# A chain of relu-squared attention and two MLPs on one core: when score chunks are left out at block ends, and in which order tokens lie

## The chip, the cores and the metric

One core of a Trainium2 chip (trn2) runs the whole program in one launch. The metric is device time in microseconds (us). TensorE (PE) multiplies, with its weight loads shown as PEld; VectorE (DVE) and ScalarE (ACT) do the elementwise work; SyncE (SP) issues nearly all DMAs.

## What is computed

Inputs u, v (4 x 3072 x 256) and z (4 x 3072 x 64) and the weights are float32. The reference, cut to what matters:

```python
scores = np.matmul(z, z.transpose(0, 2, 1)) / S          # S = 3072, 4 batches
x = u * np.matmul(np.maximum(scores, 0.0) ** 2, v)       # attention
x_prev = shift(x, 1)                                     # along the sequence
xk, xr = mu_k * x + (1 - mu_k) * x_prev, mu_r * x + (1 - mu_r) * x_prev
k = np.maximum(xk @ w_k, 0.0)
y = sigmoid(xr @ w_r) * (k * k @ w_v)                    # channel mix
out = np.maximum(y @ w_in, 0.0) ** 2 @ w_out             # second MLP
```

## The kernel before, in words

Every matrix is split into a high part, rounded to the matmul's float32r, and a low part, the rest; a product is three matmuls (high by high, and the two mixed ones). Three parts run one after the other: attention, channel mix, second MLP. The change touches attention() alone.

Attention works through 24 **blocks** `n` (4 batches `b` of 6 blocks `ib`, 512 query tokens each). A block takes 24 **steps**, one for each **chunk** of 128 key tokens; four chunks make a key group `g`. A step attends one chunk: 12 matmuls of L406, eight that read the chunk's high part (ahi) and four that read its low part (alo). Since scores are symmetric, a chunk with g < ib isn't computed again: it was turned (transposed on DVE, L335) when the earlier block made it, stored to DRAM (turned, L340 and L342), and loaded back (mixed, L351 and L353). scores(s) makes chunk s. A computed chunk takes six matmuls (sps, L374) for each two chunks, then Relu (L357), Square (L378) and a copy to ahi (L381 or L383); a turned one takes only the copy to ahi (L366). The subtraction that makes alo is handed to finish(), which holds it back until the next chunk is made (L367 and L388). So the low part of the newest chunk is put into DVE's queue only with the chunk after it.

The order of all this is written out by hand in the loop at the end of attention(). At step s it makes chunks until `made` reaches s + 1 + `ahead`, then attends chunk s:

```python
ahead = 0 if j in (NJ - 3, NJ - 2) else min(LEAD, FIRST + max(0, s - 2 * NJ) // NJ)   # FIRST 4, LEAD 7, NJ 24
while made < min(n_steps, s + 1 + ahead):
    scores(made)
```

j is the step in its block. So chunks are made 4 ahead in blocks 0 to 2, then 5, 6 and 7 ahead in blocks 3, 4 and 5, and none is made at steps 21 and 22 of any block ("left out"). At step 23 the block ends: gate() moves its four sums out of PSUM (ACT L413 and L416, DVE L420 and L418) and multiplies by u (L427); only then are three chunks made at once. Everything else (loads and preparation of z, v, u, turned scores, pieces of weights) is hung on step numbers by at_step.

z is loaded turned: load_z issues DMAs of 64 KB in rows of 128 bytes (L255). For batches 1 to 3 it loads two, DVE transposes 64 partitions (L268), and a DMA within the chip copies them to the other 64 (zT<-zT, L270). ACT then copies zz from zT (L277). In blocks 2 to 4 of a batch, and for key groups 2 to 4 (`apart`), tokens lie in another order: v goes in four DMAs of 128 KB (L288), gate() writes through a permuted view, and turned scores with i >= 2 (`spread`) are stored in four DMAs of 256 KB (L340).

SP issues its DMAs in the order of the program, and an issue that has to wait holds up those behind it.

Of the kernel before, what the change touches and what calls it, by code (L numbers as in the profile page):

```python
# [16 lines left out]
Q = 32  # L17
# [4 lines left out]
def tile_relu2_attention__rwkv_channel_mix__relu2_mlp(  # L22
# [57 lines left out]
    turned = {k: dram.tile([R, R, Q, T] if s else [R, P, T], F32, name="turned%d_%d" % k) for k, s in spread.items()}  # L80
    apart = range(2, NB - 1)
# [160 lines left out]
    def attention():  # L242
        with ExitStack() as st:
# [9 lines left out]
            def load_turned(t, p, src, g, engine=nc.sync):  # L253

                engine.dma_start(out=t[p:p + Q].rearrange("q (k r) -> q k r", r=Q),  # L255
                                 in_=src.rearrange("(q k) r -> q k r" if g in apart else "(k q) r -> q k r", q=Q))

            def load_z(b, g, engines=None):
                z_raw[b, g] = t = io.tile([P, T], F32, tag="zn", name="zn")
                for k, e in enumerate(engines or (nc.sync,) * (R if b == 0 else R // 2)):  # L260
                    d = k * Q % DQ
                    load_turned(t, k * Q, z[b, g * T:(g + 1) * T, d:d + Q], g, e)

            def prep_z(b, g, stage):
                if stage == 0:
                    rows = slice(0, P if b == 0 else DQ)
                    zT[b, g] = t = io.tile([P, T], F32, tag="zT", name="zT", bufs=1)
                    nc.vector.transpose(t[rows], z_raw.pop((b, g))[rows])  # L268
                    if b > 0:
                        nc.sync.dma_start(out=t[DQ:P], in_=t[rows])  # L270
                    return
# [9 lines left out]
            def load_v(b, g):  # L281
                src = v[b, g * T:(g + 1) * T, :]
                if g not in apart:
                    load_raw(("v", b, g), src.rearrange("(c p) d -> p c d", p=P), G, D)
                    return
                raws["v", b, g] = t = raw_p.tile([P, G, D], F32, tag="raw", name="raw")
                for k in range(R):
                    nc.sync.dma_start(out=t[k * Q:(k + 1) * Q], in_=src.rearrange("(r c k) d -> k r c d", r=Q, k=R)[k])  # L288
# [14 lines left out]
            def load_u(n, d):  # L303
                b, t0 = n // NB, (n % NB) * T
                raws["u", n, d] = t = io.tile([P, T], F32, tag="zn", name="u")
                for p in range(0, P, Q):
                    load_turned(t, p, u[b, t0:t0 + T, d * P + p:d * P + p + Q], n % NB)
# [5 lines left out]
            at, acc, ready, staged, rel, spare, late, gates = {}, {}, {}, {}, {}, {}, [], []  # L313
# [17 lines left out]
            def turn(a, i, j, c):  # L331
# [3 lines left out]
                nc.vector.transpose(t[:, :, :, c, :], a.rearrange("x (m q r) -> x q m r", m=G, q=R))  # L335
                if c == G - 1:
                    to, src = turned[i, j], t.rearrange("x q m c k -> x q (m c k)")
# [607 lines left out]
```

## Time and profile before

| what | value |
|---|---|
| median of 3 runs | 2547.32 us (2543.63 to 2548.68) |
| the profiled execution: its own time, its span | 2547.61 us, 2545.8 us |
| busy: PE, DVE, ACT | 98%, 78%, 66% of the span |
| attention | from 0 to 968 us |
| channel mix, second MLP | 968 to 1600 us, 1600 to 2546 us, PE busy 631.75 and 937.77 us |

How to read it: times in rows are us from the span's start. A row of the timeline has start, duration, engine, line, operation, what is written and read, shape and count; in brackets stands the idle time of the engine before it, and what ended it. A row of the windows has the stretch, its length, busy us (count) of PE, PEld, DVE, ACT and POOL, then PEclk, the share of time in which the 16 DMA engines were busy, and GB/s. PEclk is the granted share of TensorE's clock (1.00 is 2.4 GHz, 0.50 is 1.2 GHz), a mean over the stretch. In the timeline an SPq row is one DMA issue, or several merged.

### The profile page before, as it was taken

The numbers are of one execution on the slowest core, as the hardware profiler recorded it, in microseconds if no ns is written. First come the engines' busy times: TensorE is split into PE (matmuls) and PEld (weight loads), VectorE is DVE, ScalarE is ACT, GpSimd is POOL, SyncE is SP. The second block draws the span as 40 slices with busy tenths as digits, with TensorE's granted clock in tenths as the row PEclk, the third lists the DMA queues.
The fourth block names the chain that finished last, engine by engine and source line by source line (L and its number), as shares of the span: only waits on it lengthen the run. The fifth ranks groups of instructions, "written<-read, shape, count | busy, mean of one in ns | idle before, by whom it ended". The sixth has DMA issues, their size and how long they took to land.

```text
span 2545.8 us, 39407 instructions
## 1 busy us (share of the span) xinstructions
PE 2495.3 (98%) x14832; PEld 2061.4 (81%) x14832; DVE 1988.6 (78%) x3390; ACT 1685.1 (66%) x2943; POOL 0.2 (0%) x4
## 2 busy tenths in 40 slices
PE   7999999999999999999999999999999999999998
PEld 5787788778878878888888888788888888888887
DVE  7777787798878876888888877777777777777776
ACT  7776786697778755555655555666666666666665
POOL 0000000000000000000000000000000000000000
PEclk9999999999999999999999999999999999999999
DMA  8567758767777761212222112011110011010100
GB/s 203 150 165 196 190 160 201 185 189 192 181 194 203 172 176 61 83 63 84 82 71 87 42 67 67 18 26 25 34 34 17 18 34 34 22 29 18 34 17 17
DMA packets 304528, 244.30 MB, mean 96 GB/s; under 512 B 194385, under 2 KB 212817, under 8 KB 304337
## 3 DMA queue, kind: packets, MB, share of 16 engines
q1 hardware_dynamic: 302224, 241.39, 36.1%
q8 instruction: 116, 1.90, 0.3%
q10 hardware_dynamic: 2112, 0.39, 0.1%
q14 instruction: 76, 0.61, 0.1%
HBM read 134.50 MB, written 104.86 MB: 94 GB/s over the span
## 4 chain that ended last, share of the span: by engine, by line
PE 87%; DVE 4%; ACT 3%; DMA 2%; SPq 2%; issue 1%; DVEq 0%; ACTq 0%
PE v L406 25%; PE ups L733 16%; PE ups L208 13%; PE v L749 6%; PE v L750 6%; PE v L751 6%; PE sps L374 4%; PE v L234 3%; PE v L230 3%; PE v L231 3%; DMA mixed<-turned 1%; ACT a L357 1%; ACT a L378 1%; SPq L255 1%; SPq L351 1%
## 5 line engine op out<-in xcount | busy, mean ns | idle before, releaser
L406 PE MATMUL v<-ahi,vhl 64*128 64x512 f32 x4608 | 675.4, 391 | 6.8 <-ACT rest L416 5.5
L406 PEld LDWEIGHTS v<-ahi,vhl 64*128 64x128 f32 x4608 | 472.7, 186 | 97.4 <-ACT rest L416 10.7
L406 PE MATMUL v<-alo,vhl 64*128 64x512 f32 x2304 | 414.0, 392 | 26.0 <-DVE alo L367 18.9
L770 ACT ACTIVATE s<-s 128x512 f32<-128x512 f32 x288 | 181.3, 629 | 333.0 <-DVE s L765 332.9
L733 PE MATMUL ups<-d,win 128*128 128x512 f32 x1152 | 323.6, 389 | 0.0
L406 PEld LDWEIGHTS v<-alo,vhl 64*128 64x128 f32 x2304 | 250.4, 186 | 74.1 <-DVE alo L367 21.9
L749 PE MATMUL v<-hhi,wout 128*128 128x512 f32 x768 | 299.3, 390 | 1.0 <-ACT hhi L778 0.8
L751 PE MATMUL v<-hlo,wout 128*128 128x512 f32 x768 | 299.3, 390 | 0.4 <-DVE hlo L784 0.4
L750 PE MATMUL v<-hhi,wout 128*128 128x512 f32 x768 | 298.8, 389 | 0.0
L208 PE MATMUL ups<-mixed,wk 128*128 128x512 f32 x1152 | 291.8, 389 | 0.0
L784 DVE TENSOR_TENSOR hlo<-s,hhi 128x512 fp32r<-128x512 f32 x384 | 264.6, 689 | 22.2 <-ACT hhi L778 10.8
L160 ACT ACTIVATE a<-ups 128x512 f32<-128x512 f32 x192 | 115.1, 600 | 238.3 <-PE ups L208 231.5
L733 PEld LDWEIGHTS ups<-d,win 128*128 128x128 f32 x1152 | 216.3, 188 | 44.9
L208 PEld LDWEIGHTS ups<-mixed,wk 128*128 128x128 f32 x1152 | 216.2, 188 | 44.9
L733 PE MATMUL ups<-b,win 128*128 128x512 f32 x864 | 242.9, 389 | 0.0
L773 ACT ACTIVATE s<-s 128x512 f32<-128x512 f32 x384 | 231.6, 628 | 6.1
L357 ACT ACTIVATE a<-sps 128x512 f32<-128x512 f32 x336 | 198.6, 591 | 40.3 <-PE sps L374 36.8
L388 DVE TENSOR_TENSOR alo<-a,ahi 128x512 fp32r<-128x512 f32 x336 | 221.0, 661 | 0.0
L378 ACT ACTIVATE a<-a 128x512 f32<-128x512 f32 x336 | 213.1, 634 | 10.2
L335 DVE STREAM_TRANSPOSE turn<-a 128x512 f32<-128x512 f32 x240 | 169.4, 706 | 40.5 <-ACT a L378 35.6
L733 PEld LDWEIGHTS ups<-b,win 128*128 128x128 f32 x864 | 162.0, 188 | 34.2 <-DVE sv L765 0.8
L765 DVE TENSOR_TENSOR s<-ups,su 128x512 f32<-128x512 f32 x192 | 131.2, 683 | 58.8 <-PE ups L733 58.8
(103 smaller groups left out, 3668.0 us busy)
## 6 DMA issues: line engine op xcount, KB each, us to landing
mixed<-turned SPq DMA_DIRECT2D x220, 256.0 KB, 4.8
turned<-turn SPq DMA_DIRECT2D x36, 1024.0 KB, 5.3
turned<-turn SPq DMA_DIRECT2D x96, 256.0 KB, 4.4
u<-in_u_dram SPq DMA_DIRECT2D x192, 64.0 KB, 4.2
x2d<-xo SPq DMA_DIRECT2D x48, 256.0 KB, 2.2
x<-x2d SPq DMA_DIRECT2D x12, 1024.0 KB, 4.8
out_dram<-y SPq DMA_DIRECT2D x94, 128.0 KB, 2.8
x<-xT SPq DMA_DIRECT2D x20, 513.0 KB, 4.1
```

Of the source, the lines that this page charges most:

```text
L208: nc.tensor.matmul(ps, lhsT=lhs(h, c, f), rhs=rhs[:, m, c, :], start=k == 0, stop=k == 3 * ND - 1)
L357: nc.scalar.activation(out=a, in_=ps, func=AF.Relu, scale=1.0 / S)
L378: nc.scalar.activation(out=a, in_=a, func=AF.Square)
L388: finish(lambda: nc.vector.tensor_tensor(out=lo, in0=a, in1=hi, op=ALU.subtract))
L406: nc.tensor.matmul(acc[n, d][i], lhsT=vt[rows, k % 2, c, ds_], rhs=at[s][k // 2][rows], start=first and k == 0, stop=last and k == 2)
L733: nc.tensor.matmul(ps, lhsT=win[q][:, h, r, w], rhs=x(y), start=first and m == 0, stop=m == 2, skip_group_check=not first)
L749: nc.tensor.matmul(acc[p, b][d], lhsT=w[:, 0, c, ds_], rhs=hi, start=first, stop=False)
L750: nc.tensor.matmul(acc[p, b][d], lhsT=w[:, 1, c, ds_], rhs=hi, start=False, stop=False)
L751: nc.tensor.matmul(acc[p, b][d], lhsT=w[:, 0, c, ds_], rhs=lo, start=False, stop=last)
L770: nc.scalar.activation(out=tmp[g, c], in_=banks[g, 0] if c == "11" else tmp[g, c], func=AF.Relu, scale=HS)
L773: nc.scalar.activation(out=tmp[g, c], in_=tmp[g, c], func=AF.Square)
L784: nc.vector.tensor_tensor(out=lo, in0=tmp.pop((g, c)), in1=hi, op=ALU.subtract)
```

## The change

Two things are changed. First, `ahead` grows from 4 to 7 in block 1 (steps 30, 36 and 42 of the program) rather than over blocks 3 to 5, and steps 21 and 22 of a block are left out only where `ahead` is 7, that is in all blocks but block 0. Second, tokens lie in their natural order everywhere: v is loaded in one DMA for every group (12 of the four-part loads go), a turned store is one DMA for every pair (24 four-part stores go), gate() multiplies in place, and z of the later batches is loaded in four DMAs, without the copy zT<-zT; its three preparations stand at steps 7, 9 and 11 after the load, where they stood at 7, 11 and 13. In all 457 rows of SP's order stand where 497 stood. Shapes of matmuls and their number are the same.

```diff
...
     xT = [dram.tile([D, S], F32, name=f"xT{b}") for b in range(B)]
     R = P // Q
     spread = {(i, j): i >= 2 for j in range(NB) for i in range(j)}
-    turned = {k: dram.tile([R, R, Q, T] if s else [R, P, T], F32, name="turned%d_%d" % k) for k, s in spread.items()}
-    apart = range(2, NB - 1)
+    turned = {k: dram.tile([P, R, T] if s else [R, P, T], F32, name="turned%d_%d" % k) for k, s in spread.items()}
     def split(hi, lo, src, on_act=False):
         if on_act:
...
             ps_d = st.enter_context(tc.tile_pool(name="ps_d", bufs=1, space=PSUM))
             z_raw, zT, zz, zhi, zlo, vhl, uT = {}, {}, {}, {}, {}, {}, {}
-            def load_turned(t, p, src, g, engine=nc.sync):
+            def load_turned(t, p, src, engine=nc.sync):
                 engine.dma_start(out=t[p:p + Q].rearrange("q (k r) -> q k r", r=Q),
-                                 in_=src.rearrange("(q k) r -> q k r" if g in apart else "(k q) r -> q k r", q=Q))
+                                 in_=src.rearrange("(k q) r -> q k r", q=Q))
             def load_z(b, g, engines=None):
                 z_raw[b, g] = t = io.tile([P, T], F32, tag="zn", name="zn")
-                for k, e in enumerate(engines or (nc.sync,) * (R if b == 0 else R // 2)):
+                for k, e in enumerate(engines or (nc.sync,) * R):
                     d = k * Q % DQ
-                    load_turned(t, k * Q, z[b, g * T:(g + 1) * T, d:d + Q], g, e)
+                    load_turned(t, k * Q, z[b, g * T:(g + 1) * T, d:d + Q], e)
             def prep_z(b, g, stage):
                 if stage == 0:
-                    rows = slice(0, P if b == 0 else DQ)
-                    zT[b, g] = t = io.tile([P, T], F32, tag="zT", name="zT", bufs=1)
-                    nc.vector.transpose(t[rows], z_raw.pop((b, g))[rows])
-                    if b > 0:
-                        nc.sync.dma_start(out=t[DQ:P], in_=t[rows])
+                    zT[b, g] = io.tile([P, T], F32, tag="zT", name="zT", bufs=1)
+                    nc.vector.transpose(zT[b, g], z_raw.pop((b, g)))
                     return
                 t, k = zT[b, g], g % 2 * 2
                 if stage == 1:
...
                     nc.vector.tensor_tensor(out=zlo[b, g], in0=t, in1=zhi[b, g], op=ALU.subtract)
             def load_v(b, g):
-                src = v[b, g * T:(g + 1) * T, :]
-                if g not in apart:
-                    load_raw(("v", b, g), src.rearrange("(c p) d -> p c d", p=P), G, D)
-                    return
-                raws["v", b, g] = t = raw_p.tile([P, G, D], F32, tag="raw", name="raw")
-                for k in range(R):
-                    nc.sync.dma_start(out=t[k * Q:(k + 1) * Q], in_=src.rearrange("(r c k) d -> k r c d", r=Q, k=R)[k])
+                load_raw(("v", b, g), v[b, g * T:(g + 1) * T, :].rearrange("(c p) d -> p c d", p=P), G, D)
             def hold_v(b, g):
                 vhl[b, g] = zp.tile([P, 2, G, D], F32R, tag="vhl", name="vhl", bufs=NG)
...
                 b, t0 = n // NB, (n % NB) * T
                 raws["u", n, d] = t = io.tile([P, T], F32, tag="zn", name="u")
                 for p in range(0, P, Q):
-                    load_turned(t, p, u[b, t0:t0 + T, d * P + p:d * P + p + Q], n % NB)
+                    load_turned(t, p, u[b, t0:t0 + T, d * P + p:d * P + p + Q])
             def prep_u(n, d):
                 uT[n, d] = io.tile([P, T], F32, tag=f"uT{d}", name="uT", bufs=1)
                 nc.vector.transpose(uT[n, d], raws.pop(("u", n, d)))
-            at, acc, ready, staged, rel, spare, late, gates = {}, {}, {}, {}, {}, {}, [], []
+            at, acc, ready, staged, rel, late, gates = {}, {}, {}, {}, {}, [], []
...
                 if c == 0:
                     staged[i, j] = io.tile([P, R, G, G, Q], F32, tag="turn", name="turn")
                 t, s = staged[i, j], spread[i, j]
-                nc.vector.transpose(t[:, :, :, c, :], a.rearrange("x (m q r) -> x q m r", m=G, q=R))
+                nc.vector.transpose(t[:, :, :, c, :], a.rearrange("x (m r q) -> x q m r" if s else "x (m q r) -> x q m r",
+                                                                  m=G, q=R))
                 if c == G - 1:
-                    to, src = turned[i, j], t.rearrange("x q m c k -> x q (m c k)")
-                    if s:
-                        for p in range(R):
-                            nc.sync.dma_start(out=to[p].rearrange("q r f -> r q f"), in_=src[p * Q:(p + 1) * Q])
-                    else:
-                        nc.sync.dma_start(out=to.rearrange("q x f -> x q f"), in_=src)
+                    to = turned[i, j]
+                    nc.sync.dma_start(out=to if s else to.rearrange("q x f -> x q f"),
+                                      in_=t.rearrange("x q m c k -> x q (m c k)"))
             def load_turned_scores(n, g, k):
...
                                    zp.tile([P, R, G, G, Q], F32, tag="zz", name="zz", bufs=NG // 2))
                 to, src = ready[n, g].rearrange("y p m c k -> y p (m c k)"), turned[g, n % NB]
                 if spread[g, n % NB]:
-                    nc.sync.dma_start(out=to[:, k], in_=src[k].rearrange("q r f -> (q r) f"))
+                    nc.sync.dma_start(out=to[:, k], in_=src[k * Q:(k + 1) * Q].rearrange("r q f -> (r q) f"))
                 else:
                     nc.sync.dma_start(out=to[k * Q:(k + 1) * Q], in_=src[k].rearrange("(p r) w -> r p w", r=Q))
...
                 if d == 0:
                     rest = io.tile([P, T], F32, tag="rest", name="rest", bufs=1)
                     nc.scalar.copy(rest, halves[0])
-                    spare[n] = rest, part
                     gates.append(lambda: nc.vector.tensor_tensor(out=part, in0=rest, in1=part, op=ALU.add))
                 else:
                     nc.vector.tensor_tensor(out=part, in0=halves[0], in1=part, op=ALU.add)
                 def end():
-                    to, t_in, u_in = o, part, o
-                    if n % NB in apart:
-                        to = spare[n][d]
-                        t_in, u_in = (t.rearrange("x (k r) -> x k r", r=Q) for t in (t_in, u_in))
-                    nc.vector.tensor_tensor(out=to if to is o else to.rearrange("x (r k) -> x k r", r=Q),
-                                            in0=t_in, in1=u_in, op=ALU.mult)
-                    nc.sync.dma_start(out=xT[b][d * P:(d + 1) * P, t0:t0 + T], in_=to)
+                    nc.vector.tensor_tensor(out=o, in0=part, in1=o, op=ALU.mult)
+                    nc.sync.dma_start(out=xT[b][d * P:(d + 1) * P, t0:t0 + T], in_=o)
                 gates.append(end)
...
                     s = end + NJ * (g // 2 - 3) + 6 + 9 * (g % 2)
                     at_step(s, load_z, b, g)
                     for k in range(3):
-                        at_step(s + (7, 11, 13)[k], prep_z, b, g, k)
+                        at_step(s + 7 + 2 * k, prep_z, b, g, k)
                     s = end - NJ + G * ((g + 1) % NG) + 5
                     at_step(s - 8, load_v, b, g)
                     for h in range(2):
...
                         gate(s // NJ, 1)
                         while gates:
                             gates.pop(0)()
-                ahead = 0 if j in (NJ - 3, NJ - 2) else min(LEAD, FIRST + max(0, s - 2 * NJ) // NJ)
+                ahead = min(LEAD, FIRST + max(0, s - NJ) // 6)
+                if j in (NJ - 3, NJ - 2) and ahead == LEAD:
+                    ahead = 0
                 while made < min(n_steps, s + 1 + ahead):
                     scores(made)
                     made += 1
```

The order in which the built programs hold their instructions, at three places. Line numbers of the rows of the change are those of the changed file.

DVE at the end of block 0, before. L122 to L128 convert a piece of weights; L420, L418 and L427 are the gate; L367 makes low parts of turned chunks 24, 25 and 26 of block 1:

```order
82 L122 TENSOR_SCALAR e<-raw 128x512
83 L125 TENSOR_SCALAR e<-e 128x512
84 L128 TENSOR_SCALAR e<-e 128x512
85 L420 TENSOR_TENSOR x<-v_264,x 128x512
86 L418 TENSOR_TENSOR x<-rest,x 128x512
87 L427 TENSOR_TENSOR uT<-x,uT 128x512 x2
88 L367 TENSOR_TENSOR alo<-mixed,ahi 128x512 x3
```

The same place in the change (L407, L405 and L410 are the gate, L355 the low parts):

```order
82 L121 TENSOR_SCALAR e<-raw 128x512
83 L355 TENSOR_TENSOR alo<-mixed,ahi 128x512
84 L124 TENSOR_SCALAR e<-e 128x512
85 L355 TENSOR_TENSOR alo<-mixed,ahi 128x512
86 L127 TENSOR_SCALAR e<-e 128x512
87 L407 TENSOR_TENSOR x<-v_258,x 128x512
88 L405 TENSOR_TENSOR x<-rest,x 128x512
89 L410 TENSOR_TENSOR uT<-x,uT 128x512 x2
90 L355 TENSOR_TENSOR alo<-mixed,ahi 128x512
```

Two of the three low parts have moved ahead of the gate.

SP at the end of block 5, where v and z of the next batch are loaded, before (turned_5_107 holds turned scores):

```order
103 L255 DMA zn<-in_z_dram 32x16x32 x2
104 L351 DMA mixed<-turned_5_107 128x512 x2
105 L288 DMA raw<-in_v_dram 32x4x256 x4
106 L255 DMA u<-in_u_dram 32x16x32 x4
107 L288 DMA raw<-in_v_dram 32x4x256 x4
108 L270 DMA zT<-zT 64x512
109 L255 DMA zn<-in_z_dram 32x16x32 x2
110 L288 DMA raw<-in_v_dram 32x4x256 x4
111 L270 DMA zT<-zT 64x512
```

The same place in the change:

```order
94 L254 DMA zn<-in_z_dram 32x16x32 x4
95 L339 DMA mixed<-turned_5_107 128x512 x2
96 L93 DMA raw<-in_v_dram 128x4x256
97 L254 DMA u<-in_u_dram 32x16x32 x4
98 L93 DMA raw<-in_v_dram 128x4x256
99 L254 DMA zn<-in_z_dram 32x16x32 x4
100 L93 DMA raw<-in_v_dram 128x4x256
```

24 issues stood there, 17 stand there now; two more z loads come ahead of the turned scores.

ACT at the same place, before (L366 makes high parts of turned chunks, L301 those of v, L277 those of z; L357 begins the computed chunks of block 6):

```order
273 L366 CAST ahi<-mixed 128x512 x2
274 L301 CAST vhl<-raw 128x512
275 L366 CAST ahi<-mixed 128x512 x2
276 L301 CAST vhl<-raw 128x512
277 L277 CAST zz<-zT 128x512
278 L357 ACTIVATE a<-sps 128x512
```

The same place in the change:

```order
272 L354 CAST ahi<-mixed 128x512 x2
273 L291 CAST vhl<-raw 128x512
274 L273 CAST zz<-zT 128x512
275 L354 CAST ahi<-mixed 128x512 x2
276 L291 CAST vhl<-raw 128x512
277 L345 ACTIVATE a<-sps 128x512
```

The copy of zz stands two turned chunks and one copy of v earlier.

## Rows read from the trace of the kernel before

**Rows 1.** The page: busy time of each engine, share, instructions.

```profile
PE 2495.3 (98%) x14832; PEld 2061.4 (81%) x14832; DVE 1988.6 (78%) x3390; ACT 1685.1 (66%) x2943; POOL 0.2 (0%) x4
```

**Rows 2.** Windows of blocks 0 to 5, 7, 8 and 10 (columns: see above).

```profile
11.30:64.00 52.70, 46.69 (x353) 34.79 (x351) 44.76 (x80) 41.40 (x76) 0.00 (x0) 0.94 0.78 208
64.00:107.30 43.30, 40.49 (x346) 35.94 (x342) 33.00 (x57) 33.79 (x59) 0.00 (x0) 0.96 0.58 158
107.30:150.70 43.40, 40.00 (x338) 36.60 (x336) 31.39 (x54) 30.66 (x53) 0.00 (x0) 0.96 0.63 158
150.70:193.60 42.90, 38.76 (x327) 36.18 (x326) 32.59 (x57) 27.56 (x48) 0.00 (x0) 0.96 0.71 163
193.60:234.20 40.60, 37.17 (x327) 30.22 (x326) 31.61 (x56) 25.78 (x46) 0.00 (x0) 1.00 0.75 171
234.20:277.00 42.80, 37.99 (x316) 29.98 (x314) 28.10 (x47) 24.41 (x45) 0.00 (x0) 0.96 0.73 181
...
318.80:357.00 38.20, 38.20 (x339) 31.42 (x335) 32.05 (x56) 33.02 (x58) 0.00 (x0) 1.00 0.66 187
357.00:395.50 38.50, 38.50 (x339) 34.41 (x338) 30.46 (x53) 30.23 (x52) 0.00 (x0) 1.00 0.66 163
...
432.60:469.70 37.10, 37.10 (x328) 30.19 (x326) 30.63 (x54) 25.15 (x45) 0.00 (x0) 1.00 0.80 186
```

**Rows 3.** Timeline of PE, blocks 0 to 5: rows behind idle time.

```profile
54.63 1.22 PE L406 MATMUL v<-alo,vhl 64*128 64x512 f32 x4 [3.94 <-DVE alo L388]
...
67.38 0.79 PE L406 MATMUL v<-alo,vhl 64*128 64x512 f32 x2 [2.81 <-DVE alo L367]
...
111.38 0.76 PE L406 MATMUL v<-alo,vhl 64*128 64x512 f32 x2 [3.40 <-DVE alo L367]
...
155.58 0.61 PE L406 MATMUL v<-alo,vhl 64*128 64x512 f32 x2 [4.14 <-DVE alo L367]
...
198.46 0.51 PE L406 MATMUL v<-alo,vhl 64*128 64x512 f32 x2 [3.43 <-DVE alo L367]
...
239.43 0.74 PE L406 MATMUL v<-alo,vhl 64*128 64x512 f32 x4 [1.11 <-DVE alo L388]
```

**Rows 4.** Timeline of DVE, start of block 1, just behind the gate.

```profile
66.64 1.89 DVE L367 TENSOR_TENSOR alo<-mixed,ahi 128x512 fp32r<-128x512 f32 x3
```

**Rows 5.** Waits: engine, line, what it waited for, us in total, times, longest.

```profile
ACT zz L277 <- DMA zT<-zT: 40.0, 10, 6.9
```

**Rows 6.** Timeline of all engines, end of block 5.

```profile
259.16 0.70 DVE L268 STREAM_TRANSPOSE zT<-zn 64x512 f32<-64x512 f32 x1 [3.49 <-DMA zn<-in_z_dram]
...
266.14 0.54 SPq L270 DMA_DIRECT2D zT<-zT  x1
...
269.20 0.62 ACT L277 CAST zz<-zT 128x512 fp32r<-128x512 f32 x1 [4.10 <-DMA zT<-zT]
```

**Rows 7.** Timeline of PE where blocks 5, 11 and 17 end.

```profile
272.09 0.79 PE L406 MATMUL v<-alo,vhl 64*128 64x512 f32 x2 [3.54 <-DVE alo L367]
...
504.13 0.50 PE L406 MATMUL v<-alo,vhl 64*128 64x512 f32 x2 [1.56 <-DVE alo L367]
509.05 0.73 PE L406 MATMUL v<-ahi,vhl 64*128 64x512 f32 x4 [1.67 <-ACT rest L416]
...
739.57 0.73 PE L406 MATMUL v<-ahi,vhl 64*128 64x512 f32 x4 [1.62 <-ACT rest L416]
```

**Rows 8.** Timeline of all engines in block 0.

```profile
29.55 2.50 SPq L288 DMA_DIRECT2D raw<-in_v_dram  x4
...
53.29 0.71 DVE L335 STREAM_TRANSPOSE turn<-a 128x512 f32<-128x512 f32 x1 [3.71 <-DMA turned<-turn]
```

**Rows 9.** Timeline of all engines at the end of block 22.

```profile
923.58 2.85 SPq L340 DMA_DIRECT2D turned<-turn  x4
...
934.40 0.73 PE L406 MATMUL v<-ahi,vhl 64*128 64x512 f32 x4 [2.04 <-ACT rest L416]
```

**Rows 10.** DMA issues by line: count, KB each, median us from issue to landing.

```profile
zn<-in_z_dram SPq DMA_DIRECT2D x58, 64.0 KB, 3.7
```

## Prediction, made before the changed kernel was run

> **What bounds the kernel.** I read four views in this order. The page says that PE is busy for 98% of the span [rows 1], so a change gains only where PE stands idle or runs at the lower clock. The windows, one to a block of attention, show where that is [rows 2]: in blocks 7, 8 and 10 PE is busy for the whole of the window, at PEclk 1.00; in blocks 0 to 5 it is not. The reader compares block 2 with block 8, which do the same work: 43.4 against 38.5 us. The timeline of PE gives each idle time and what ended it [rows 3, 7], and the timelines of DVE, ACT and SP tell why that one was late [rows 4, 6, 8, 9]. Behind attention PE is busy without a break (631.75 of the channel mix's 632 us, by the table above), so what attention gains the kernel gains.
>
> PEclk in a window prices the clock: (1 - 0.96) x 43.3 = 1.7 us are lost in block 1, the same 1.7 in blocks 2, 3 and 5, and (1 - 0.94) x 52.7 = 3.2 us in block 0 [rows 2]. Each of these blocks has an idle time of PE ahead of its stretch at 1.2 GHz: 2.81, 3.40, 4.14, 3.54 and 3.94 us [rows 3, 7]. Block 4 has 3.43 us idle and no loss of clock, so a loss isn't certain even there.
>
> **Term A, the leave-out, 19.6 us.** At the start of block 1 PE waits 2.81 us for a low part [rows 3]. The row of DVE shows it: three low parts are made at 66.64, behind the gate, and the wait ends at 67.38 [rows 4]. They stood there because nothing is made at steps 21 and 22, and finish() holds each low part back until the next chunk is made. With chunks made 4 ahead, the one held back is the first that the new block needs; with 5 it is the second, with 6 the third. The traces agree: PE idles at the start of blocks 2 and 3 (3.40 and 4.14 us, 4 ahead at the end before), of block 4 (3.43, 5 ahead), and, further in, of block 5 (1.11, 6 ahead) [rows 3]. With 7 ahead it is the fourth, and the starts of blocks 7, 8 and 10 are without idle time [rows 2].
>
> The change has 7 ahead from step 42, so the starts of blocks 2 to 5 become like those of 8 and 10. For block 1 the order shows two of the three low parts ahead of the gate. The third is for the third chunk of the block; it takes the place at 66.64 and is done some 0.7 us later (1.89 for three that overlap), while PE has two chunks and some scores to work on. I take the whole 2.81 as gone. Sum: 2.81 + 3.40 + 4.14 + 3.43 + 1.11 = 14.9 us idle, plus 0.04 x (43.3 + 43.4 + 42.9) = 5.2 of clock in blocks 1 to 3: 20.1 us. A check by windows: block 2 less block 8 is 4.9 (3.40 + 1.7 by the sum), block 4 less block 10 is 3.5 (3.43).
>
> What it may cost: the lead of three chunks must be built in block 1 while ACT is well filled. Block 7 has the same shape and 7 ahead, with ACT busy 33.02 of 38.20 us and no idle PE [rows 2]. Block 1 has ACT busy 33.79; without its idle time and its loss of clock it would last 43.3 - 2.8 - 1.7 = 38.8 us. The room is 5 us, and the three chunks gained are turned ones of block 2, which take ACT one copy each (the timeline's zz copy, of the same shape, takes 0.62 [rows 6]): 1.9 us. They fit. The bounds are 0 and the 7.3 of the second rival; I take 0.5 us, near the lower, since the room is more than twice the need. A = 20.1 - 0.5 = 19.6.
>
> **Term B, the copy of z, 9.1 us.** ACT waits 40.0 us in ten places for zT<-zT [rows 5]. Most is off the path, as PE has chunks in hand; at the end of a batch it is not. At the end of block 5 DVE turns z at 259.16, done at 259.86; the copy is issued only at 266.14, because SP stood behind the loads of u and the four-part loads of v; ACT's zz waits 4.10 us for it until 269.20, all later chunks wait behind that in ACT's queue, and PE stands still for 3.54 us [rows 6, 7]. Blocks 11 and 17 end alike: PE idles 1.56 and 1.67 us about the end of the one, 1.62 about that of the other [rows 7]. The change has no such copy, and its zz depends on DVE's transpose alone. Sum 3.54 + 1.7 (clock of block 5) + 1.56 + 1.67 + 1.62 = 10.1.
>
> Against it: z now takes four loads, not two, and DVE waits for them; it waited 3.49 us in block 5 already, without idle PE behind it [rows 6]. The turned scores stand behind these loads in SP's queue. Two more loads at 0.63 us of issue each (2.50 for four equal issues [rows 8]) are 1.3 us; the cover of this wait is between 3.49 us, which was absorbed, and an end that no row shows. Per batch 0 to 1.3 us; I take 0.3, nearest to what was absorbed, together 1.0. B = 9.1.
>
> **Term C, block 22, 1.4 us.** PE idles 2.04 us where block 23 starts [rows 9]. ACT there waits, by its timeline, for a load of x that SP issues behind the four stores, which take 2.85 us. One store in place of four, at 2.85 / 4 = 0.7 us, lets the load go 2.1 us earlier. Bounds 0 and 2.04; I take two thirds, since the load still follows as many bytes.
>
> **Term D, block 0, 3.0 us.** PE idles 3.94 us because DVE waited 3.71 us for a turned store to land before it could reuse the staging buffer [rows 3, 8], and 3.2 us of clock follow. These stores are not split and don't change. But SP is ahead of them with fewer issues: the four-part load of v took 2.50 us [rows 8], one issue of four costs 0.63, so 1.9 us are saved ahead of them. The store still waits for its data and for a DMA queue that is busy 78% of the block [rows 2]. Bounds 0 and 7.1; I take 1.4 us of the idle time and half the clock's cost, 1.6.
>
> The Trainium skill has a rule against counting C and D: its page "DMA: Bandwidth & Descriptors", section "Issuing engines are not separate DMA queues", holds that the time a sequencer takes to initiate a DMA is usually small beside the DMA itself. By that rule C and D would be nil, and the sum 28.7, the time 2518.9 us. The row speaks against it here: 2.50 us to issue 512 KB [rows 8].
>
> **At nothing.** The gate's products through a permuted view become plain, and DVE's transposes of z cover 128 partitions, not 64: DVE is busy 27 to 38 us of each block [rows 2], and its work here lies beside PE's. Natural order moves the same bytes in rows of the same size for u, v and z. If turned stores in one DMA landed late, DVE would wait for a staging buffer as in block 0, with 7 chunks in hand in its stead.
>
> **Sum.** 19.6 + 9.1 + 1.4 + 3.0 = 33.1 us off the profiled execution's 2547.6, which lies 0.3 us above the median of the runs: 2514.5 us.
>
> **The rivals.** First, the relief of the queues is complete: A loses nothing, B and C come whole, block 0 loses all its idle time and its stretch at 1.2 GHz: 20.1 + 10.1 + 2.0 + 7.1 = 39.3, time 2508.3. For it speaks that each late transfer of these rows stands behind others on SP; against it, that the DMA engines are well filled in block 0.
>
> Second, the lead isn't built cheaply in block 1. ACT falls behind, and PE, which makes the scores in order, stops for its Relus. That gives back block 1's gain, 2.8 + 1.7, and the time in which ACT makes up for two chunks, at 33.79 / 24 = 1.4 us each [rows 2]: 7.3 us, time 2521.8. The room of 5 us speaks against it.
>
> Third, four loads of z in rows of 128 bytes are slower than two and a copy on the chip. They land so late that term B is eaten up: 2523.6. A load of z takes 3.7 us to land at the median [rows 10]. The same page of the Trainium skill, section "Specifications", says that a transfer wants runs of at least 512 bytes for full rate; that would speak for this rival, and no run here yet shows how four such loads go.
>
> Fourth, the other side: the same mechanism, but without cover. If landing takes twice as long with twice the loads, DVE waits 3.7 us more for each of 18 groups of z, and with a cover c it costs PE 18 x (3.7 - c). With B nil the gain is 24.0, so the change is slower than before where c is below 3.7 - 24.0 / 18 = 2.4 us; at c = 1.7 the cost is 36 and the time 2560. Against it: 3.49 us were absorbed [rows 6].
>
> Fifth, that the change does not do what it says, the starts of blocks 1 to 5 staying as they are, would give 2534 with B to D; the starts of blocks 7 and 8 make that unlikely.
>
> **How the numbers follow.** Forecast 0.56 (2510 to 2519), first rival 0.16, second 0.12, third 0.09, fourth 0.03, fifth 0.02, and 0.02 for no change. The range reaches from 2505, as small idle times inside blocks may go along with the first rival, to 2526, which holds the second and third; about 0.15 lie outside. A measurement of this kernel can tell about 0.2%, 5 us, from no change. Faster by more than that: 0.95, the first five cases without the fourth. Within: 0.02. Slower: 0.03.
>
> **What would show it.** In the profile after, right: the windows of blocks 1 to 4 last about 39, 38.5, 37 and 37 us with PEclk 1.00; no low part of a turned chunk ends an idle time of PE at their starts; zT<-zT is gone from the waits, and block 5 lasts about 36.5 us. Block 0 between 45 and 53 us tells how much of D came. Wrong: "PE sps <- ACT a" grows in block 1 (second rival), or DVE's waits for zn grow above 4 us with idle PE behind them (third, fourth). The prediction fails if attention ends after 945 us, where it ended at 968.

## The result, and the profile after

The changed kernel takes 2508.97 us (median of 4 runs, 2508.6 to 2509.49). The kernel before took 2547.32 us, the median of three runs; a fourth, of 4520 us, stands far from all others and is left out. The ratio is 0.9853, 95% interval [0.9833, 0.9872]. The profiled executions took 2547.6 us before and 2508.6 after (span 2506.8): 39.0 us off where 33.1 were forecast. The time lies inside the range, but 1 us below the 2510 to 2519 of the forecast itself, and 0.7 us from the first rival's 2508.3.

The page after, busy time of each engine [before: rows 1]:

```profile
PE 2484.7 (99%) x14832; PEld 2037.2 (81%) x14832; DVE 2014.7 (80%) x3390; ACT 1682.6 (67%) x2943; POOL 0.2 (0%) x4
```

PE's instructions are the same in number; its busy time fell by 10.6 us, 9.0 of it in blocks 0 to 5 (windows below). Most of it goes with the lower clock: the five blocks that had a stretch at 1.2 GHz lost 1.5 to 2.1 us of busy time each, block 4, which had none, 0.07. DVE has the same number of instructions too and is busy 26.1 us more, which the prediction did not have (last section).

Windows after, columns as in [rows 2]: blocks 0 to 5, then 11, 17 and 22.

```profile
11.40:61.10 49.70, 44.89 (x353) 32.76 (x351) 45.75 (x82) 42.41 (x78) 0.00 (x0) 1.00 0.81 217
61.10:99.80 38.70, 38.70 (x344) 31.82 (x340) 32.69 (x57) 33.97 (x60) 0.00 (x0) 1.00 0.63 180
99.80:138.30 38.50, 38.50 (x340) 31.38 (x338) 36.34 (x57) 30.24 (x53) 0.00 (x0) 1.00 0.72 192
138.30:175.30 37.00, 37.00 (x326) 30.15 (x326) 33.96 (x56) 27.02 (x47) 0.00 (x0) 1.00 0.80 192
175.30:212.40 37.10, 37.10 (x328) 30.23 (x326) 31.84 (x55) 25.41 (x45) 0.00 (x0) 1.00 0.87 185
212.40:248.30 35.90, 35.87 (x316) 29.05 (x314) 27.13 (x46) 23.67 (x44) 0.00 (x0) 1.00 0.84 209
...
440.70:476.40 35.70, 35.70 (x316) 29.23 (x316) 28.51 (x48) 24.70 (x45) 0.00 (x0) 1.00 0.83 211
...
668.00:703.70 35.70, 35.70 (x314) 29.26 (x314) 27.36 (x47) 23.91 (x44) 0.00 (x0) 1.00 0.81 209
...
858.80:895.80 37.00, 37.00 (x326) 30.15 (x324) 29.72 (x52) 25.13 (x44) 0.00 (x0) 1.00 0.70 171
```

Compare with [rows 2]: blocks 1 to 4 were 43.3, 43.4, 42.9 and 40.6 us, PE idle for some 3 us in each, PEclk 0.96 in three of them. Now PE is busy for the whole of blocks 1 to 4, at PEclk 1.00. Block 5 went from 42.8 to 35.9. Attention ends at 929.02 us, where it ended at 967.65: 38.6 of the 39.0 us were gained there.

Block lengths, from the first matmul of a block's attending to that of the next, in us:

| block | before | after | gain |
|---|---|---|---|
| 0 | 52.67 | 49.65 | 3.0 |
| 1 to 4 | 170.24 | 151.31 | 18.9 |
| 5, 6 | 84.55 | 77.46 | 7.1 |
| 7 to 10 | 150.91 | 150.85 | 0.1 |
| 11, 12 | 81.13 | 76.48 | 4.7 |
| 17, 18 | 79.57 | 76.98 | 2.6 |
| 22 | 39.31 | 37.07 | 2.2 |

Blocks 7 to 10, where PE had no idle time to lose, kept their lengths. At the end of block 5, after, on all engines [before: rows 6]:

```profile
227.15 4.02 SPq L254 DMA_DIRECT2D zn<-in_z_dram  x4
...
234.85 0.71 DVE L266 STREAM_TRANSPOSE zT<-zn 128x512 f32<-128x512 f32 x1 [3.11 <-DMA zn<-in_z_dram]
...
238.92 0.61 ACT L273 CAST zz<-zT 128x512 fp32r<-128x512 f32 x1
```

Between DVE's transpose and ACT's copy lay 10 us and a wait of 4.10 us [rows 6]; now 4 us, and ACT does not wait. In the waits of the kernel after, the 40.0 us for zT<-zT [rows 5] are gone and these stand for z:

```profile
DVE zT L266 <- DMA zn<-in_z_dram: 12.4, 4, 4.8
...
ACT zz L273 <- DVE zT L266: 6.4, 5, 2.5
```

### The profile page after: what moved, and what is told of

Same layout as the page of the kernel before. It is cut to its first block, busy times and chain, and to the rows that moved or that the text cites. A ratio compares the mean times of both kernels' runs of the same rounds, so it can differ in the third digit from the quotient of the medians.

```text
span 2506.8 us, 39271 instructions
## 1 busy us (share of the span) xinstructions
PE 2484.7 (99%) x14832; PEld 2037.2 (81%) x14832; DVE 2014.7 (80%) x3390; ACT 1682.6 (67%) x2943; POOL 0.2 (0%) x4
## 4 chain that ended last, share of the span: by engine, by line
PE 92%; ACT 3%; DVE 3%; DMA 1%; issue 1%; SPq 0%; DVEq 0%; ACTq 0%
PE v L394 27%; PE ups L717 17%; PE ups L207 13%; PE v L733 7%; PE v L735 7%; PE v L734 7%; PE sps L362 4%; PE v L230 3%; PE v L233 3%; PE v L229 3%; ACT a L345 1%; ACT a L366 1%; DMA turned<-turn 0%; ACT vhl L291 0%; DVE alo L376 0%
## 5 line engine op out<-in xcount | busy, mean ns | idle before, releaser
L394 PE MATMUL v<-ahi,vhl 64*128 64x512 f32 x4608 | 666.8, 388 | 0.0
L394 PEld LDWEIGHTS v<-ahi,vhl 64*128 64x128 f32 x4608 | 459.2, 184 | 98.0 <-DVE x L407 5.9
L394 PE MATMUL v<-alo,vhl 64*128 64x512 f32 x2304 | 407.5, 388 | 4.8 <-DVE alo L376 4.2
L394 PEld LDWEIGHTS v<-alo,vhl 64*128 64x128 f32 x2304 | 243.5, 184 | 55.4 <-DVE alo L376 11.2
L325 DVE STREAM_TRANSPOSE turn<-a 128x512 f32<-128x512 f32 x240 | 206.8, 862 | 24.4 <-ACT a L366 19.7
L366 ACT ACTIVATE a<-a 128x512 f32<-128x512 f32 x336 | 212.7, 633 | 10.2
```

The costliest lines, as they stand in the source:

```text
L325: nc.vector.transpose(t[:, :, :, c, :], a.rearrange("x (m r q) -> x q m r" if s else "x (m q r) -> x q m r", m=G, q=R))
L366: nc.scalar.activation(out=a, in_=a, func=AF.Square)
L394: nc.tensor.matmul(acc[n, d][i], lhsT=vt[rows, k % 2, c, ds_], rhs=at[s][k // 2][rows], start=first and k == 0, stop=last and k == 2)
```

## The experiments

Twelve kernels ran, each timed against the kernel before on its chip (medians there 2548.0, 2546.3 and 2546.9). "After" is the changed kernel; when it ran once more among the last four, it took 2508.8. Lengths of blocks come from one profiled execution of each kernel.

| kernel | us | ratio to before, 95% interval |
|---|---|---|
| before, new rule for the lead alone | 2527.6 | 0.9919 [0.9904, 0.9934] |
| after, old rule for the lead | 2528.2 | 0.9921 [0.9906, 0.9936] |
| before, z in four loads without copy | 2539.9 | 0.9968 [0.9955, 0.998] |
| after, copy of z back | 2517.8 | 0.9878 [0.9863, 0.9892] |
| after, v in four DMAs | 2513.2 | 0.9864 [0.9842, 0.9885] |
| after, turned stores in four DMAs | 2513.4 | 0.9866 [0.9844, 0.9888] |
| after, z prepared later | 2511.1 | 0.9856 [0.9834, 0.9877] |
| after, left out at block 0's end too | 2516.3 | 0.9876 [0.9851, 0.9902] |
| after, never left out | 2512.2 | 0.9863 [0.985, 0.9877] |
| after, again | 2508.8 | 0.9852 [0.9839, 0.9866] |
| after, weights loaded later | 2508.9 | 0.9849 [0.9836, 0.9863] |
| after, weights and u loaded later | 2507.3 | 0.9845 [0.9832, 0.9859] |

### The two halves of the change

The lead alone, on the kernel before; the second kernel is the reverse, the kernel after with the old line:

```diff
-                ahead = 0 if j in (NJ - 3, NJ - 2) else min(LEAD, FIRST + max(0, s - 2 * NJ) // NJ)
+                ahead = min(LEAD, FIRST + max(0, s - NJ) // 6)
+                if j in (NJ - 3, NJ - 2) and ahead == LEAD:
+                    ahead = 0
```

> The kernel before with the new rule for ahead alone; tokens, stores and loads as before. If the lead alone removes the idle time at the starts of blocks 1 to 5 (theory, term A), attention loses the 20 us that blocks 1 to 4 and the start of block 5 got shorter by: 2528 us, blocks 1 to 4 last 38.8, 38.4, 37.1 and 37.1 us, and blocks 0, 11, 12, 17 and 22 keep the lengths of before (52.7, 39.4, 41.8, 37.9, 39.3). Rival, that the shorter SP queue is what let the lead be built: 2535 us or more, with idle time of PE left at these starts.

> The changed kernel with the old rule for ahead: natural order of tokens, fewer DMAs, no copy of z. Theory (terms B, C, D): 2548 - 19 = 2529 us, idle time of 3 to 4 us left at the starts of blocks 1 to 4, none at the ends of blocks 5, 11, 17 and 22. Rival, that the two parts only work together: 2540 us or more.

The lead alone gives 20.4 us, the rest alone 19.9; together 40.3 against the 39.0 of both, so the two parts nearly add up. The blocks do not split as I expected, though. With the lead alone blocks 1 to 4 are 18.8 us shorter, but block 5 is 4.2 shorter and not 1.1, and blocks 17 and 23 last 39.36 and 34.51 us, 1.5 and 1.3 longer than before, though the edit leaves their steps alone. So the length of a single block near the end of a batch can differ by 1 to 1.5 us without a cause in its own steps. Windows of blocks 1 and 2 with the lead alone:

```profile
64.00:102.80 38.80, 38.80 (x346) 31.92 (x344) 32.87 (x57) 33.85 (x59) 0.00 (x0) 1.00 0.62 180
102.80:141.30 38.50, 38.50 (x338) 34.52 (x338) 31.86 (x56) 30.25 (x53) 0.00 (x0) 1.00 0.71 179
```

With the old rule in the kernel after, the old idle times come back to 0.01 us at the starts of blocks 1 and 2 [rows 3], and for the most part at those of blocks 3 and 4 (3.43 and 2.69 us). PE's timeline:

```profile
65.22 0.80 PE L394 MATMUL v<-alo,vhl 64*128 64x512 f32 x2 [2.81 <-DVE alo L355]
...
110.64 0.50 PE L394 MATMUL v<-alo,vhl 64*128 64x512 f32 x2 [3.39 <-DVE alo L355]
```

### z without the copy, and with it

z alone, on the kernel before (load_z also issues four loads there, not shown); the other kernel puts the copy, two loads and the old steps 7, 11, 13 back into the kernel after:

```diff
-                    rows = slice(0, P if b == 0 else DQ)
...
-                    nc.vector.transpose(t[rows], z_raw.pop((b, g))[rows])
-                    if b > 0:
-                        nc.sync.dma_start(out=t[DQ:P], in_=t[rows])
+                    nc.vector.transpose(zT[b, g], z_raw.pop((b, g)))
```

> The kernel before with z loaded in four DMAs and no copy zT<-zT; all else as before, its four-part loads of v too. Theory (the copy is what came late at the ends of batches): blocks 5, 11, 12, 17 and 18 lose the 13 us by which they got shorter in the change: 2535 us. Rival, that the four-part loads of v held up the queue and the copy only suffered from it: DVE now waits for z in its place, a gain under 4 us, 2544 us or more.

> The changed kernel with two z loads and the copy zT<-zT put back, its preparations at 7, 11 and 13 steps as before. Theory (the copy): 13 us are given back, 2522 us, with zT<-zT ending PE's waits at the ends of blocks 5, 11 and 17. Rival (the queue): the copy is issued on time now that v is one DMA, 2509 to 2512 us.

Without the copy the kernel before gains 8.1 us; with it the kernel after loses 8.8, both between the two expectations. So the copy is worth 8 to 9 us at most, and not the 13 by which the ends of batches became shorter; the 8.8 also hold the later preparation, which cost 2.2 when it was set back alone (below). What the copy does not explain stands at the end of block 17, where four loads alone gain nothing: it lasts 39.24 us there, with 2.83 us of idle PE. That is 1.4 longer than before, but about as long as with the lead alone (39.36, with 3.2 us of idle PE). Timeline of all engines there, of the kernel before with four loads of z:

```profile
707.43 3.85 SPq L255 DMA_DIRECT2D zn<-in_z_dram  x4
711.32 2.99 SPq L348 DMA_DIRECT2D mixed<-turned  x2
714.41 2.49 SPq L285 DMA_DIRECT2D raw<-in_v_dram  x4
...
715.35 0.71 DVE L267 STREAM_TRANSPOSE zT<-zn 128x512 f32<-128x512 f32 x1 [3.65 <-DMA zn<-in_z_dram]
...
718.80 1.14 ACT L363 CAST ahi<-mixed 128x512 fp32r<-128x512 f32 x2 [5.51 <-DMA raw<-in_v_dram]
...
724.82 0.50 PE L403 MATMUL v<-alo,vhl 64*128 64x512 f32 x2 [1.15 <-DVE alo L364]
```

z is in time there, and ACT waits 5.51 us. The row names a load of v, but the cast reads turned scores (mixed), and the first of these v loads landed only at 718.97, after the cast had begun. The second of the two loads of turned scores was issued at 713.30 and landed at 718.62, 0.18 us before the cast: that is what ACT waited for. On SP it stood behind the four loads of z, which took 3.85 us to issue. So with the copy gone, the turned scores are late next. That four loads of z are to blame for it is not shown, since the lead alone, with two loads and the copy, leaves as much idle time here. In the kernel after with the copy back, the same place shows the copy's own way to fail:

```profile
690.27 6.30 SPq L254 DMA_DIRECT2D u<-in_u_dram  x4
...
698.27 0.47 SPq L269 DMA_DIRECT2D zT<-zT  x1
...
704.06 0.62 ACT L276 CAST zz<-zT 128x512 fp32r<-128x512 f32 x1 [4.36 <-DMA zT<-zT]
...
706.96 0.51 PE L397 MATMUL v<-alo,vhl 64*128 64x512 f32 x2 [1.66 <-DVE alo L358]
```

### v and the turned stores in four DMAs, z prepared later

The bytes, their order in memory and every other step are those of the kernel after; v of groups 2 to 4 is loaded in four DMAs (the other groups keep the old line), or turned scores with i >= 2 stored in four:

```diff
-                load_raw(("v", b, g), v[b, g * T:(g + 1) * T, :].rearrange("(c p) d -> p c d", p=P), G, D)
+                for k in range(R):
+                    nc.sync.dma_start(out=t[k * Q:(k + 1) * Q], in_=src[k * Q:(k + 1) * Q])
```

```diff
-                    nc.sync.dma_start(out=to if s else to.rearrange("q x f -> x q f"),
-                                      in_=t.rearrange("x q m c k -> x q (m c k)"))
+                    src = t.rearrange("x q m c k -> x q (m c k)")
+                    if s:
+                        for p in range(R):
+                            nc.sync.dma_start(out=to[p * Q:(p + 1) * Q], in_=src[p * Q:(p + 1) * Q])
```

> The changed kernel with v of groups 2 to 4 in four DMAs again, in natural order. The copy of z alone explained 8 to 9 of the 13 us that the ends of batches gained. Theory: the rest, 4 us, is what the issues of v took of SP's time ahead of u, z and the turned scores, and block 0 loses another 1 to 2 us: 2513 to 2515 us, blocks 5, 11 and 17 longer by 1 us or more each. Rival, that the same bytes make the same wait however they are issued: 2509 to 2510 us.

> The changed kernel with turned stores of pairs with i >= 2 in four DMAs again, in natural order. Theory (term C): block 22 gets its 2.2 us back, as the load of x waits behind four issues, the rest stays: 2511 us. Rival, that block 22 gained from the cheaper gate or the v loads: 2509 us, block 22 at 37.1 us.

v in four costs 4.2 us: block 0 is 2.7 us longer (52.35), block 17 1.1 and block 22 0.7. Blocks 5 and 11, which I expected 1 us longer too, kept their lengths (35.69 and 35.71). So one DMA for v is worth more in block 0 than at the ends of batches. The idle time of block 0 is back, close to [rows 3, 8] and with 1.2 GHz behind it:

```profile
53.37 0.71 DVE L331 STREAM_TRANSPOSE turn<-a 128x512 f32<-128x512 f32 x1 [3.80 <-DMA turned<-turn]
...
54.71 1.16 PE L400 MATMUL v<-alo,vhl 64*128 64x512 f32 x4 [3.65 <-DVE alo L382]
```

The stores in four cost 4.4 us, 2 more than I expected: 2.0 in block 22, 1.4 in block 23 (part of it now at 1.2 GHz), 0.9 in block 0, which differs by 0.4 between the two profiles of after. In block 22 SP needs 2.71 us for the four, so the load of x goes out late and lands late:

```profile
888.02 2.71 SPq L331 DMA_DIRECT2D turned<-turn  x4
890.77 1.15 SPq L178 DMA_DIRECT2D x<-xT  x1
...
896.91 0.72 ACT L188 ACTIVATE m<-x,om 128x512 f32<-128x512 f32 x1 [4.46 <-DMA x<-xT]
...
898.64 0.73 PE L397 MATMUL v<-ahi,vhl 64*128 64x512 f32 x4 [1.85 <-ACT rest L407]
```

In the kernel after the store takes 0.34 us of SP, the load is issued 0.39 us behind the start of the store and not 2.75, and PE has no idle time there:

```profile
887.23 0.34 SPq L329 DMA_DIRECT2D turned<-turn  x1
887.62 0.43 SPq L178 DMA_DIRECT2D x<-xT  x1
```

The intervals of both ratios overlap with that of after. The times do not (lowest 2511.83 and 2512.29 us, highest of after's eight runs 2511.26), and the rows show where most of the cost lies.

Last, the steps at which z is prepared (now 7, 9, 11) were set back:

```diff
-                        at_step(s + 7 + 2 * k, prep_z, b, g, k)
+                        at_step(s + (7, 11, 13)[k], prep_z, b, g, k)
```

> The changed kernel with the preparations of z at 7, 11 and 13 steps after the load, as before, in place of 7, 9 and 11. Theory: without the copy zT is ready by either step, so nothing: 2509 us. Rival, that taking zz out of ACT's queue just ahead of the new batch's first chunks was part of the gain: blocks 5, 6, 11, 12, 17 and 18 get 0.5 us or more longer each, 2512 us or more.

2511.1 us, 2.2 above after. Blocks 17 and 18 are 1.8 us longer together, with 1.24 us of idle PE in block 17; blocks 5, 6 and 11, where the rival wanted 0.5 us or more, are not longer. The intervals of the two ratios overlap, so the size is not settled; the place is the one where z alone gained nothing.

### Where to leave out

One kernel leaves out at block 0's end too (the old rule there, the new one behind it), one never:

```diff
-                if j in (NJ - 3, NJ - 2) and ahead == LEAD:
+                if j in (NJ - 3, NJ - 2):
```

> The changed kernel with steps 21 and 22 of block 0 left out too, with 4 chunks ahead there. Theory: two low parts stand behind the gate again, PE idles 2.8 us at the start of block 1, 2512 us, and up to 2514 us if the clock falls behind it. Rival, that the lead built later in block 1 makes up for it or the gate is earlier: 2509 us.

> The changed kernel with no step left out anywhere. Theory: with 7 ahead the held-back low part is the seventh of a block, so nothing is late for want of it; but the copies and products of the gate now stand behind two more chunks on ACT and DVE, the sums leave PSUM later, and PE waits for ACT's copy (L404) at the starts of computed blocks: 2509 to 2520 us, losses where blocks begin with computed chunks (6, 12, 18). Rival, that leaving out is useless with 7 ahead: 2509 us or less.

In the first, block 1 is 41.89 us, 3.1 longer, and begins as it did before [rows 3, 4]. Timelines of PE and DVE:

```profile
65.06 0.50 PE L394 MATMUL v<-alo,vhl 64*128 64x512 f32 x2 [2.79 <-DVE alo L355]
```

```profile
63.10 1.29 DVE L410 TENSOR_TENSOR uT<-x,uT 128x512 f32<-128x512 f32 x2
64.31 1.89 DVE L355 TENSOR_TENSOR alo<-mixed,ahi 128x512 fp32r<-128x512 f32 x3
```

The low parts stand behind the gate again; this one edit shows term A's mechanism by itself. Its profiled execution is 5.9 us above that of after: 3.1 in block 1, and 0.7 to 0.8 in each of blocks 0, 11 and 12. Only the first has to do with the edit as far as the trace shows (block 12 lasts 40.77 or 41.26 in other kernels that leave it alone). The median is 7.3 above, more than I expected, and the rest of it is not explained.

Never leaving out costs 3.4 us, but not where I expected it. Of blocks 6, 12 and 18, which I thought would suffer, 12 and 18 are 1.2 and 1.7 us shorter (39.60, 39.59); block 6 lasts 41.16 us, with PEclk at 0.96 behind the idle time shown below. The loss is at other ends, 3.2 us in block 5, 1.5 in block 17, 1.0 in block 2, 1.1 in block 0. PE at the end of block 5 waits for the gate's copy (L404), which now stands in ACT's queue behind the chunks made at steps 21 and 22:

```profile
253.49 1.15 PE L394 MATMUL v<-ahi,vhl 64*128 64x512 f32 x4 [2.71 <-ACT rest L404]
```

### What is left in block 0

Two kernels take other loads out of the way of block 0's turned stores: the first piece of weights four steps later, and with it the second load of u three steps later.

```diff
-                at_step(steps[0] - 10, load_raw, ("w", i), src, src.shape[1], src.shape[2])
+                at_step(steps[0] - (6 if i == 0 else 10), load_raw, ("w", i), src, src.shape[1], src.shape[2])
```

> The changed kernel again, as the yardstick for the three beside it: 2509 us, blocks 0 and 1 at 49.7 and 38.8 us.

> The changed kernel with the first piece of weights loaded 4 steps later, so that it doesn't stand ahead of the turned store that DVE waits for in block 0. Theory (term D: block 0 waits for a store behind other bytes): DVE's wait of 1.5 us for the store goes, block 0 gets up to 1.5 us shorter, 2507.5 to 2508.5 us. Rival, that DVE itself limits block 0 and the idle time moves: 2509 us.

> The same, and the second load of u in block 0 three steps later too, so that 256 KB more in rows of 128 bytes stand behind the store. Theory: as x9_wk_later with no wait of DVE left, 2507 to 2508.5 us. Rival: 2509 us, or more, if u is now late for its transpose.

Block 0 lasts 50.03 us in the repetition of after, 48.93 with the weights later, 48.48 with u later too; DVE's wait for the store goes from 1.83 us to 0.79 and then to none. So the wait for the store is for loads that stand ahead of it. The whole time follows less: with the weights later alone it is 2508.85 us against 2508.8, where the rival had it, as blocks 6 and 22 are 0.8 and 0.4 us longer in that profile. The last of the three is the fastest kernel of the study, 2507.3 us (5 runs, 2506.16 to 2508.53), 1.5 below the repetition of after; the intervals overlap, so it is not shown to be faster.

## Why the prediction was right, and where its terms were not

**Bound and method.** PE bounds attention, and gains came only where PE stood idle or at the lower clock. That held in every kernel; blocks 7 to 10 kept their lengths within 0.2 us.

**Term A: right, in mechanism and size.** Blocks 1 to 4 gained 18.9 us and block 5's early idle time of 1.11 is gone: 20.0 where 19.6 were forecast. (The lead alone gave 20.4, but only 18.8 of it in blocks 1 to 4; the rest is the balance of gains and losses in blocks 5, 17 and 23.) The deduction of 0.5 for building the lead in block 1 was not needed: block 1 lasts 38.76 us against the 38.8 worked out, with ACT busy 33.97 us.

**Term B: right place, mis-sized.** The ends of batches gained 13.2 us (blocks 5, 6, 11, 12, 17, 18 without that 1.11) where 9.1 were forecast; this is 4.1 of the 5.9 us missed. Two steps failed. The deduction of 1.0 for four loads of z did not come: DVE waits 12.4 us in all for them, in four places, where it waited 10.9 in four before, and PE has chunks in hand. And the 10.1 counted only the idle times of 1.5 us and more. Block 12 has one window before and one after:

```profile
509.10:550.80 41.70, 40.43 (x349) 32.52 (x350) 37.84 (x68) 36.17 (x64) 0.00 (x0) 1.00 0.76 218
```

```profile
476.40:517.20 40.80, 40.21 (x351) 32.98 (x349) 36.40 (x65) 35.27 (x63) 0.00 (x0) 1.00 0.76 220
```

Its idle time of 1.27 us is now 0.6; the same in block 18 (0.6 less) and block 6 (0.5): 1.8 us in small pieces, and the rest in matmuls that follow each other a little closer. (Block 6 lasts 40.77 us in some of these kernels and 41.5 in others, so a piece of this size is only known to within some 0.8.) I also gave the whole of it to the copy. The copy is worth 8 to 9 at most. Of the other 4, put back one at a time, v in four DMAs costs these six blocks 1.0 us and the later preparation of z 1.2, both near what a single block varies by; some 2 us have no experiment of their own.

**Term C: right, its size too small.** 2.2 us came where 1.4 were forecast, and with the stores in four 2.0 of it went back. I had taken two thirds, because the load follows as many bytes either way; it landed in time all the same.

**Term D: the sum right, in part by luck.** 3.0 us came as forecast. I had 1.4 of idle time and 1.6 of clock; by the windows of block 0, PE's idle time fell by 1.2 us (6.01 to 4.81) and its busy time by 1.8 (46.69 to 44.89). But they came in another way. PE after, in block 0:

```profile
52.53 0.73 PE L394 MATMUL v<-alo,vhl 64*128 64x512 f32 x4 [1.72 <-DVE alo L376]
...
57.98 0.50 PE L394 MATMUL v<-alo,vhl 64*128 64x512 f32 x2 [0.93 <-DVE alo L376]
```

The idle time of 3.94 us fell to 1.72, a new one of 0.93 stands behind it, and the stretch at 1.2 GHz is wholly gone, where I had taken half. So the whole stretch was worth 1.8 us of busy time, and not the 3.2 at which I priced it by PEclk. That half of 3.2 comes near 1.8 is luck. The windows of the stretch at the lower clock before and of the like one after suggest why it was worth less:

```profile
55.00:60.00 5.00, 5.00 (x26) 3.87 (x26) 5.00 (x10) 1.41 (x3) 0.00 (x0) 0.50 0.51 188
```

```profile
52.00:57.00 5.00, 4.33 (x32) 2.77 (x32) 5.00 (x10) 3.35 (x6) 0.00 (x0) 1.00 0.71 257
```

DVE is busy 5.00 of 5.00 us in both, with ten instructions. At the full clock PE does 32 matmuls there and not 26, far from twice as many, and idles 0.67 us. My reading is that DVE sets the pace there, so that the lost clock was worth less than PEclk says; no run took DVE's load away to test it.

**The rule weighed against C and D.** It would have made C and D nil. The runs differ: splitting the same bytes into four issues cost 2.7 us in block 0 for v (4.2 in all) and 2.0 in block 22 for the turned stores (4.4 in all). The Trainium skill ("DMA: Bandwidth & Descriptors", section "Issuing engines are not separate DMA queues") calls the time to initiate a DMA usually small beside the DMA; here SP's order is fixed, and what counts is the time that a late transfer's issue stood behind others.

**At nothing: one cost missed.** Natural order is not free on DVE (below). It was hidden.

**The rivals.** The first was nearest in time, nearer than the forecast's own 2514.5, and in A, B and C also in kind; block 0 did not lose all its idle time. The second, third and fourth did not come: block 1 has no idle PE, and no idle time of PE goes back to z. The fourth had its cover, as DVE's longest wait for z is 4.8 us and PE did not stop. By the prediction's own sign (attention over by 945) it held: 929.

## What to carry to other kernels

Where an engine makes work some steps ahead and holds back the newest piece, ask which piece the next stage needs first; here a pause in making it cost idle time with 4, 5 and 6 chunks ahead, and none with 7. With one queue that issues in program order, count the issues ahead of each late transfer, since splitting a DMA delays all behind it. And do not stop at the largest waits at one place: if several share a cause, the small ones go along, and the next late transfer shows up once the first is gone. When a row names a transfer as the end of a wait, check that the waiting instruction reads it and that it had landed by then.

## What the runs showed of the hardware that was not expected

**Transposes that read in steps of 16 bytes.** The page's groups for DVE's transposes of scores, before and after:

```profile
L335 DVE STREAM_TRANSPOSE turn<-a 128x512 f32<-128x512 f32 x240 | 169.4, 706 | 40.5 <-ACT a L378 35.6 <-DMA turned<-turn 4.2
```

```profile
L325 DVE STREAM_TRANSPOSE turn<-a 128x512 f32<-128x512 f32 x240 | 206.8, 862 | 24.4 <-ACT a L366 19.7 <-DMA turned<-turn 1.5
```

In block 2 alone, where all twelve read through the new view (every fourth element, 16 bytes apart), after:

```profile
L325 DVE STREAM_TRANSPOSE turn<-a 128x512 f32<-128x512 f32 x12 | 13.3, 1109 | 0.4
```

They took 708 ns there before. With 96 such transposes that is 96 x 0.40 = 38 us more on DVE; the plain products of the gate give about 9 back (24 at some 0.69 in place of 1.07 us), and DVE's total is 26 us higher. It costs nothing here, since PE is busy for all of block 2, but DVE now fills 36.34 of its 38.5 us. The Trainium skill ("SBUF — State Buffer", section "Door 1: The DMA port swizzle") says that reading on within a 16-byte line is at full rate and each step to a new line pays; the row agrees, at 1109 against 708 ns.

**The clock after an idle time.** 3.43 us of idle PE ahead of block 4 cost no clock before, and 3.40 ahead of block 2 did [rows 3]. The same 2.04 us of idle PE ahead of block 23, in the same place, cost none before and did with the lead alone. Windows of block 23, before and with the lead alone:

```profile
934.40:967.60 33.20, 33.20 (x289) 26.79 (x289) 27.06 (x44) 15.63 (x28) 0.00 (x0) 1.00 0.45 128
```

```profile
912.50:947.00 34.50, 34.49 (x289) 28.96 (x289) 27.06 (x44) 15.95 (x28) 0.00 (x0) 0.95 0.45 123
```

So idle time of one length came both with and without a fall of the clock, and no run here tells what decides it. The 1.4 us of block 23 with the stores in four, behind 1.85 us of idle PE, are of this kind, so they may not come in every execution.
